# Block 0's attention logits: one product and three split sums instead of eight products, with q, k in strided feature groups

## The chip, the cores and the metric

The kernel runs on one core of a Trainium2 chip. The metric is the device time of one execution in microseconds (us), the median of several runs. Each engine has its own in-order queue: TensorE (PE, with its weight loads PEld), VectorE (DVE), ScalarE (ACT), GpSimd (POOL), and SyncE (SP), which here only issues DMAs.

## The reference, cut to what matters

Two layer types are applied twice each: local attention A, then a gated MLP B (x is 2048 x 1024, 32 heads of 32 features, 8 window positions at a step of 2).

```python
x = x + _A_ref(_layernorm(x), wqkv, wo)
x = x + _B_ref(_layernorm(x), W_gate, W_up, W_down)
...
qkv = (x @ wqkv).reshape(B, S, 3, H, Dh)
idx = pos[:, None] - arange(8) * 2
logits = einsum("bhsd,bhswd->bhsw", q, kg) * scale
o = einsum("bhsw,bhswd->bhsd", softmax(masked logits), vg)
```

A logit is a sum over the 32 features of a head: q of a position times k of the position 0, 2, ... 14 earlier.

## The kernel before, in words

The sequence is cut into four blocks of 512 positions (BLK); a block is four tiles of 128 positions. All order is written by a planner (class Plan, L48). It keeps a plan time for TensorE (`plan.pe`, 0.216 us for each 512-column matmul), puts VectorE's attention chain and its short fixed operations in one order with given durations (`_place_dve`), gives the weight slabs their ring slots (`_place_slabs`), and in the end issues everything sorted by plan time. ACT, POOL and SP have no clock of their own in the plan: their instructions stand in their queues in the order of plan times. Each engine works its queue in order, and an instruction waits for its operands.

**Order on TensorE.** At the start `First` (L278) normalizes block 0 tile by tile while the first slab's matmuls run on finished tiles. Then come the projections of blocks 0 to 3 (`plan_proj`, L354), each six slabs of 512 columns (q, k, v; two halves g), each slab four accumulators j of 128 features x 512 positions, each accumulator 8 matmuls over kc (L364). Between them stands wo of block 0 (`plan_wo`, L633, after block 2), then the MLPs with the other wo's, and layers 2 and 3 in the same way.

**Evictions.** A projection's accumulator is copied to SBUF by ACT (L373) and stored to DRAM in pairs of accumulators (L378, L381, issued from ACT); later the head-major q, k and v are loaded from there by SP (`load`, L492). Block 0's q and k are the exception: `first_logits` (L421) keeps them feature-major in SBUF (`q_fm`, `k_fm`, L433 and L436), so that the logits need no trip to DRAM.

**Block 0's logits before.** For each group c of 128 consecutive features (4 heads), VectorE multiplies q by the eight shifted k (L451: 128 x 4096 bf16). TensorE sums over the features: with a 128 x 32 matrix of ones, cut from `wide` so that group c lands in its 4 head rows, each product takes 8 matmuls (L464), 64 for the eight products, in two lots of 32 (after the first q tile of the second half, and inside block 1's q). They add up in two PSUM banks, which ACT copies out (L473) for the softmax (`soft_a`, `expo`, `soft_b`, L533 to L556).

**Around it.** LayerNorm of block b+1 runs beside the projections of block b (`late_ln`, `plan_ln`, L206): per tile two sums on ACT (L219, L220; S4 to S7 for block 1's tiles and S8 to S11 for block 2's in the text), small operations on VectorE (L226 to L238) and POOL (L233), one normalization on ACT (L244; N4 to N11), and one DMA transpose for two tiles on SP (L250). After the softmax VectorE makes block 0's output in eight groups (L563 to L573), POOL stores each (L574), SP loads it transposed (`load_o`, L582) and TensorE multiplies it by wo (L642).

**Weights.** Layer 0's six slabs stay in SBUF for all four blocks: q's and k's first halves and q's second in `held` (L777, the buffer of the later hT), the rest in the ring of five slots (L190). They are loaded in the order q0 v0 k0 v1 q1 k1, x's tiles between (L785, L771).

Of the kernel before, what the change touches and what calls it, by code (L numbers as in the profile page):

```python
# [14 lines left out]
P = 128  # L15
D = 1024
H = 32
# [13 lines left out]
NG = DH // DG  # L31

# [15 lines left out]
class Plan:  # L48
# [3 lines left out]
    def __init__(self, slots):  # L52
        self.steps = []
        self.pe = 0.0
        self.fixed = []
        self.chain = []
        self.ring = []
        self.slots = slots
        self.n = 0
# [4 lines left out]
    def on_pe(self, n, fn, slabs=()):  # L64
        t = self.pe
        self.at(t, fn)
        self.pe = t + n * MM
        for s in slabs:
            s["last"] = self.pe
        return self.pe  # L70
# [33 lines left out]
    def _place_slabs(self):  # L104
        free = [-10.0] * self.slots
        for s in self.ring:
            free.sort()
            t = max(free.pop(0), s["start"])
            self.at(t + 0.01, s["load"])
            free.append(s["last"])  # L110
# [9 lines left out]
def kernel(  # L120
# [31 lines left out]
    wring = ctx.enter_context(tc.tile_pool(name="wring", bufs=RING))  # L152
# [13 lines left out]
    wide = const.tile([P, 60], BF16, name="wide")  # L166
# [12 lines left out]
    def consts_late():  # L179
        nc.gpsimd.memset(wide[:], 0.0)  # L180
        for hl in range(4):
            nc.gpsimd.memset(wide[32 * hl:32 * hl + 32, 28 + hl:29 + hl], 1.0)
        nc.gpsimd.memset(zpad[:], 0.0)
        for t in (v_d, k_d):
            nc.gpsimd.dma_start(_dram(t[0], 0, [[ROW, P], [P * ROW, KC], [1, HALO]]), zpad[:])
        nc.gpsimd.memset(maskc[:], 0.0)
        for w in range(1, W):
            nc.gpsimd.memset(maskc[:, w, 0:DIL * w], NEG)

    def slab(src_ap, name, start=-10.0):  # L190
        shp = list(src_ap.shape)

        def load():
            t = wring.tile([P, 8, SLAB], BF16, tag="slab", name=name)
            s["t"] = t[:, 0:shp[1], 0:shp[2]]
            nc.sync.dma_start(s["t"], src_ap)

        s = plan.slab(load, start)
        return s
# [154 lines left out]
    def plan_proj(L, b, hooks={}):  # L354
# [3 lines left out]
        def mms(nm, g, j, w, t0=0, t1=TPB, k0=0, k1=KC):  # L358
            def f():
                if t0 == 0 and k0 == 0:  # L360
                    hold[(nm, g, j)] = psum.tile([P, BLK], F32, tag="acc", name=f"acc_{nm}")
                acc = hold[(nm, g, j)]
                for kc in range(k0, k1):
                    nc.tensor.matmul(acc[:, t0 * P:t1 * P], lhsT=w["t"][:, kc, j * P:(j + 1) * P],  # L364
                                     rhs=xnT[(L, b)][:, t0:t1, kc, :], start=(kc == 0), stop=(kc == KC - 1))
            return f
# [20 lines left out]
        tiles = []  # L387
        if L == 0 and b == 0:

            first = First()  # L390
            plan.at(-1.0, first.begin)
            tiles = [("q", 0, j) for j in range(4)]
            for t in range(TPB - 1):
                for h, (nm, g, j) in ((h, x) for h in range(2) for x in tiles):
                    plan.on_pe(1, mms(nm, g, j, w0[(nm, g)], t, t + 1, KC // 2 * h, KC // 2 * (h + 1)), [w0[(nm, g)]])
                    if h == 1 and j == 2:
                        e = plan.on_pe(2, lambda t=t: first.turn(t + 1))
                        plan.at(e, lambda t=t: first.copies(t + 1))
        order = "q0 k0 q1 k1 v0 v1" if "evict" not in hooks else "q0 v0 k0 v1 q1 k1"
        for nm, g in ((o[0], int(o[1])) for o in order.split()):  # L400
            if L == 0:
                w = w0[(nm, g)]
            else:
                col0 = "qkv".index(nm) * D + g * SLAB
                w = slab(wqkv_v[:, :, col0:col0 + SLAB], f"w{nm}_{L}_{b}_{g}")
            for j in range(4):
                if (nm, g, j) in tiles:
                    e = plan.on_pe(2, mms(nm, g, j, w, TPB - 1, TPB), [w])
                else:
                    e = plan.on_pe(8, mms(nm, g, j, w), [w])  # L410
                if "evict" in hooks and nm != "v":
                    hooks["evict"](nm, 4 * g + j, lambda k=(nm, g, j): hold.pop(k), e + T_EV)
                else:
                    plan.at(e + T_EV, evict(nm, g, j))
                if (nm, g, j) in hooks:
                    hooks[(nm, g, j)]()
            ends[nm] = e
        return ends


    def first_logits(st, tm):  # L421
        hold = {}
        Ls = []
# [6 lines left out]
        def evict(nm, c, acc, t):  # L430
            def f():
                if nm == "q":
                    nc.scalar.copy(hold["q"][:, c, :], acc()[:])  # L433
                    return
                kt = hold["k"]
                nc.scalar.copy(kt[:, c, HALO:HALO + BLK], acc()[:])  # L436
                nc.gpsimd.dma_start(_dram(k_d[1], c * P * ROW, [[ROW, P], [1, HALO]]), kt[:, c, BLK:BLK + HALO])
            if nm == "q" and c == 0:
                plan.at(t - 1.0, begin)
            plan.at(t, f)  # L440
            if nm == "k":
                plan.chain.append((lambda: max(t + 0.7, reds.get(c - 4, 0.0) + 0.1), 2.25, mul(c),
                                   (lambda n: tm.__setitem__("logits", n)) if c == KC - 1 else None))

        def mul(c):
            def f():
                if c % 4 < 2:
                    pr = at_pool.tile([P, W, BLK], BF16, tag="pr", name=f"prod_{c}", bufs=2)
                else:
                    pr = tpose.tile([P, W, BLK], BF16, tag="T", name=f"prod_{c}")  # L450
# [5 lines left out]
        def red(c0, n):  # L456
            def f():
                if c0 == 0:
                    Ls.extend(psum.tile([P, 4, P], F32, tag="acc", name=f"L{wh}") for wh in range(2))
                for c in range(c0, c0 + n):  # L460
                    pr = hold.pop(("pr", c))
                    for wh in range(2):
                        for tq in range(TPB):
                            nc.tensor.matmul(Ls[wh][32 * tq:32 * tq + 32, :, :], lhsT=wide[:, 28 - 4 * c:60 - 4 * c],  # L464
                                             rhs=pr[:, 4 * wh:4 * wh + 4, tq * P:(tq + 1) * P],
                                             start=(c == 0), stop=(c == KC - 1),
                                             skip_group_check=True, tile_position=(0, 32 * tq))
            return f

        def out():  # L470
            st["L"] = at_pool.tile([P, W, P], F32, tag="L", name="L_0_0")
            for wh in range(2):
                nc.scalar.copy(st["L"][:, 4 * wh:4 * wh + 4, :], Ls[wh][:])  # L473

        reds = {}

        def step(c0, n):
            def f():
                e = plan.on_pe(1.0 + 2.25 * n, red(c0, n))
                for c in range(c0, c0 + n):  # L480
                    reds[c] = e
                if c0 + n == KC:
                    plan.at(e + T_EV, out)
                    tm["logits_in"] = e + T_EV + 1.5
            return f

        return {"evict": evict, ("q", 1, 0): step(0, 4)}, {("q", 0, 2): step(4, 4)}


    def plan_attn(L, b, ends, st, tm):  # L490
# [106 lines left out]
        def v_ready():  # L597
            t = ends["v"] + 6.0
            if prev:
                t = max(t, prev[-1]["pv"] + 0.5, tm["qk_in"] + 10.0)  # L600
# [17 lines left out]
        def after_pv(t):  # L618
            tm["pv"] = t
            t = max(t + 5.0, st["wo_at"] - 30.0)  # L620
            step = 3.0 if first else PIECE
# [79 lines left out]
    def plan_down(L, b, st, last):  # L701
# [21 lines left out]
        def add(half, t, c0, n):  # L723
            def f():
# [3 lines left out]
                if end:  # L728
                    eng = nc.scalar if t == 1 or (t == TPB - 1 and c0 == SLAB) else nc.sync
                    eng.dma_start(out_dram[r0:r0 + P, c0:c0 + n], xt[:, c0:c0 + n])  # L730
                elif last and half == 1:
                    nc.sync.dma_start(out_dram[r0:r0 + P, :], xt[:])
# [19 lines left out]
    later_hooks = []  # L752

    def proj(L, b):
# [3 lines left out]
        else:  # L758
            hooks = later_hooks.pop() if later_hooks else {}
# [17 lines left out]
    held = hT_pool.tile([P, FC, BLK], BF16, tag="hT", name="wqk_0")  # L777
    for i, (nm, g) in enumerate((("q", 0), ("v", 0), ("k", 0), ("v", 1), ("q", 1), ("k", 1))):
        col0 = "qkv".index(nm) * D + g * SLAB
        if i % 2 == 0:  # L780
            w0[(nm, g)] = {"t": held[:, 4 * i:4 * i + 8, :], "last": 0.0}
            pieces = ((0, KC // 2), (KC // 2, KC)) if i == 0 else ((0, KC),)
            for h, (a, z) in enumerate(pieces):
                plan.at(-7.0 + i + 0.6 * h, lambda w=w0[(nm, g)], a=a, z=z, c=col0:
                        nc.sync.dma_start(w["t"][:, a:z, :], wqkv_v[:, a:z, c:c + SLAB]))  # L785
        else:
            w0[(nm, g)] = slab(wqkv_v[:, :, col0:col0 + SLAB], f"w{nm}_0_{g}", -7.0 + i)
# [7 lines left out]
    for b in range(NB):  # L795
        if b + 1 < NB:
            late_ln(0, b + 1, plan.pe + 9.0, 0.5 if b == 0 else 8.0)
        if b == NB - 1:
            wo(0, 0)
# [56 lines left out]
```

## Time and profile before

| what | us |
|---|---|
| median of 3 runs (1622.80 to 1623.27) | 1623.18 |
| the profiled execution | 1622.84 |
| its span, first to last instruction | 1621.10 |
| TensorE busy in it | 1611.6 |
| reduction of block 0's logits on TensorE, 64 matmuls (chain of waits) | 2 x 1.84 |
| VectorE's eight products, first start to last end | 29.5 to 59.3 |
| ACT busy from 62.70 to 84.85 | 19.67 of 22.15, 33 instructions |
| a group of 32 projection matmuls (chain of waits) | 6.91 |

How to read the profile: the page gives each engine's busy time, the span in 40 slices, and the chain of work that ended last. Groups of instructions are given by line of the kernel, engine, operation and operands (out<-in, partitions x elements). The timeline lists instructions in order of time: start, length, engine, line, operation, and in brackets the idle time before it with what ended it. An instruction's length is not its pitch: matmuls of 379 ns follow each other every 216 ns, and rows of ACT and VectorE can overlap by some 0.1 us.

### The profile page before, as it was taken

What the parts mean: (1) busy time and instruction counts of PE and PEld (TensorE: products, weight loads), DVE (VectorE), ACT (ScalarE), POOL (GpSimd) and SP (SyncE); (2) the same over time, 40 slices, a digit from 0 to 9 for tenths busy, and PEclk for the clock granted to TensorE, in tenths of its full rate; (3) what the DMA queues carried; (4) which work ended last, traced back from release to release, by engine and by line L of the source; (5) the groups of instructions that cost most, each with busy time, mean ns of one, the idle gap of its engine ahead of it and who ended that gap; (6) DMA issues with size and microseconds to landing.
All of it is one profiled execution on the core that took longest, in us unless ns stands there. A gap on an engine that the chain in (4) does not pass through costs nothing.

```text
span 1621.1 us, 19223 instructions
## 1 busy us (share of the span) xinstructions
PE 1611.6 (99%) x7641; PEld 740.6 (46%) x7690; DVE 1014.6 (63%) x1256; ACT 458.1 (28%) x735; POOL 109.3 (7%) x174
## 2 busy tenths in 40 slices
PE   9999999999999999999999999999999999999999
PEld 5444444444444444444444444444444444444444
DVE  4576999989989069960699616986989212211211
ACT  6564421304131241312413251133011311221110
POOL 3221000001001100011000110000000000000000
PEclk9999999999999999999999999999999999999999
DMA  8799798597866988669876699599846655565452
GB/s 240 163 199 192 191 218 210 167 217 193 219 173 211 223 206 208 188 200 234 202 198 196 213 223 226 158 279 240 216 154 194 172 182 162 176 173 165 156 167 67
DMA packets 444203, 314.83 MB, mean 194 GB/s; under 512 B 195504, under 2 KB 438608, under 8 KB 444112
## 3 DMA queue, kind: packets, MB, share of 16 engines
q1 hardware_dynamic: 414944, 281.39, 66.7%
q10 hardware_dynamic: 24368, 23.40, 4.7%
q0 software_dynamic: 4800, 8.80, 1.8%
q8 instruction: 60, 0.98, 0.3%
q14 instruction: 31, 0.25, 0.1%
HBM read 261.77 MB, written 36.05 MB: 184 GB/s over the span
## 4 chain that ended last, share of the span: by engine, by line
PE 99%; DMA 0%; DVE 0%; issue 0%; SPq 0%; POOL 0%; DVEq 0%; POOLq 0%
PE acc_g L672 24%; PE acc_u L672 24%; PE dacc L718 24%; PE acc_v L364 7%; PE acc_k L364 7%; PE acc_wo L642 7%; PE acc_q L364 7%; DMA x<-in_A_x_dram 0%; PE L L464 0%; DVE bst L294 0%; POOL rstd L318 0%; DVE xn_all L323 0%; DVE x L726 0%; SPq L785 0%; DVE xnT L331 0%
## 5 line engine op out<-in xcount | busy, mean ns | idle before, releaser
L672 PE MATMUL acc_u<-xnT,wu 128*128 128x512 bf16 x1792 | 423.3, 379 | 0.0
L672 PE MATMUL acc_g<-xnT,wg 128*128 128x512 bf16 x1792 | 423.3, 379 | 0.0
L718 PE MATMUL dacc<-wd,hT 128*128 128x512 bf16 (+1 forms) x1787 | 386.4, 376 | 1.7
L687 DVE TENSOR_TENSOR hT<-acc_u,r 128x512 bf16<-128x512 f32 x224 | 154.1, 688 | 323.9 <-PE acc_u L672 318.3
L679 ACT ACTIVATE r<-acc_g 128x512 bf16<-128x512 f32 x224 | 133.3, 596 | 711.9 <-PE acc_g L672 700.3
L718 PEld LDWEIGHTS <-hT 128*128 128x128 bf16 x1820 | 178.1, 98 | 209.0
L672 PEld LDWEIGHTS <-wu 128*128 128x128 bf16 x1792 | 175.3, 98 | 211.4
L672 PEld LDWEIGHTS <-wg 128*128 128x128 bf16 x1792 | 175.3, 98 | 211.5
L512 DVE TENSOR_TENSOR pr<-qhm,khm 128x4096 bf16<-128x4096 bf16 x56 | 127.9, 2284 | 30.7 <-DMA khm<-k_d 30.6
L563 DVE TENSOR_TENSOR pvt<-a,vhm 128x4096 bf16<-128x4096 bf16 x64 | 146.2, 2285 | 0.2
L522 DVE TENSOR_TENSOR l<-l,pr 128x1024 f32<-128x1024 f32 x112 | 136.8, 1221 | 2.2
L726 DVE TENSOR_TENSOR x<-dacc,x 128x512 bf16<-128x512 f32 (+1 forms) x65 | 43.2, 681 | 126.1 <-PE dacc L718 125.9
L364 PE MATMUL acc_v<-xnT,wv 128*128 128x512 bf16 x512 | 112.0, 379 | 0.0
L642 PE MATMUL acc_wo<-wo,oT 128*128 128x512 bf16 x496 | 111.0, 379 | 0.8
L364 PE MATMUL acc_k<-xnT,wk 128*128 128x512 bf16 x384 | 84.8, 379 | 0.0
L219 ACT ACTIVATE xn_all<-x 128x1024 bf16<-128x1024 bf16 x60 | 63.3, 1055 | 73.8 <-DVE x L649 71.0
L571 DVE TENSOR_TENSOR pvt<-pvt 128x2048 bf16<-128x2048 bf16 x64 | 78.1, 1221 | 1.3
L373 ACT CAST stage_q<-acc_q 128x512 bf16<-128x512 f32 x56 | 32.0, 582 | 162.1 <-PE acc_q L364 153.3
L642 PEld LDWEIGHTS <-oT 128*128 128x128 bf16 x512 | 50.1, 98 | 60.4
L364 PEld LDWEIGHTS <-wv 128*128 128x128 bf16 x512 | 50.1, 98 | 60.2
L244 ACT ACTIVATE xn_all<-x,nb,rstd 128x1024 bf16<-128x1024 bf16 x60 | 71.9, 1233 | 14.2 <-DVE nb L238 11.2
L574 POOL DMA_DIRECT2D o_d<-ohm x64 | 35.2, 550 | 599.7 <-DVE ohm L573 581.7
(76 smaller groups left out, 883.1 us busy)
## 6 DMA issues: line engine op xcount, KB each, us to landing
wg<-in_B_W_gate_dram SPq DMA_DIRECT2D x56, 1024.0 KB, 7.2
wu<-in_B_W_up_dram SPq DMA_DIRECT2D x56, 1024.0 KB, 5.4
wd<-in_B_W_down_dram SPq DMA_DIRECT2D x48, 1024.0 KB, 6.4
wo<-in_A_wo_dram SPq DMA_DIRECT2D x16, 1024.0 KB, 6.9
wv<-in_A_wqkv_dram SPq DMA_DIRECT2D x10, 1024.0 KB, 5.7
wk<-in_A_wqkv_dram SPq DMA_DIRECT2D x9, 1024.0 KB, 5.0
vhm<-v_d SPq DMA_DIRECT2D x32, 284.0 KB, 7.0
v_d<-stage_v ACTq DMA_DIRECT2D x32, 256.0 KB, 6.8
```

What stands on the lines that cost most here:

```text
L219: nc.scalar.activation(junk, xt[:], ACT.Identity, accum_out=st[:, 0, t % 2:t % 2 + 1])
L244: nc.scalar.activation(hold["xn"][:, t, :], x_tiles[b * TPB + t][:], ACT.Identity, scale=rstd[:, i:i + 1], bias=nb[:, i:i + 1])
L364: nc.tensor.matmul(acc[:, t0 * P:t1 * P], lhsT=w["t"][:, kc, j * P:(j + 1) * P], rhs=xnT[(L, b)][:, t0:t1, kc, :], start=(kc == 0), stop=( ...
L512: nc.vector.tensor_tensor(pr[:], st["q"][:], _ap(st["k"], HALO - DIL * w, [[HALO + P, DH], [1, P]]), op=ALU.mult)
L522: nc.vector.tensor_tensor(l[:], pr[:, 0:8] if i == 0 else l[:], pr[:, 8 * i + 8:8 * i + 16], op=ALU.add)
L563: nc.vector.tensor_tensor(tt[:], a_bc, v_sh, op=ALU.mult)
L571: nc.vector.tensor_tensor(tt[:, 0:4], tt[:, 0:4], tt[:, 4:8], op=ALU.add)
L642: nc.tensor.matmul(acc[:], lhsT=st["oT"][:, c, t, :], rhs=ws[half]["t"][:, c, :], start=(c == 0), stop=(c == KC - 1))
L672: nc.tensor.matmul(acc[:], lhsT=w["t"][:, kc, (j % 4) * P:(j % 4 + 1) * P], rhs=xnT[(L, b)][:, :, kc, :], start=(kc == 0), stop=(kc == KC ...
L679: nc.scalar.activation(r[:], hold.pop(("g", j))[:], ACT.Relu)
L687: nc.vector.tensor_tensor(st["hT"][:, j, :], hold.pop(("u", j))[:], hold.pop(("r", j))[:], op=ALU.mult)
L718: nc.tensor.matmul(accs[(t, c0)][:], lhsT=st["hT"][:, j, t * P:(t + 1) * P], rhs=w["t"][:, jl, c0 - half * SLAB:c0 - half * SLAB + n], sta ...
```

## The change: what it does

1. In block 0, group c of q and k now holds every eighth feature: c, c+8, c+16, ... (the weights are read by TensorE with a step of eight columns). Partition p of every group then belongs to head p // 4, so products of different groups may be added partition by partition.
2. VectorE adds the products of groups 0 to 6 in f32 (two halves of 128 x 2048, `lacc`), and splits the sum into three bf16 terms: ACT copies it to bf16 (term_0), VectorE subtracts, ACT copies the rest (term_1), VectorE subtracts again (term_2). TensorE sums the last product (group 7) and the three terms with one 128 x 32 matrix: 32 matmuls in one lot, placed after the second v tile of block 1. The terms take the buffers of the products, of k_fm and of q_fm.
3. Block 0's order is v's first half, then q and k group by group, then v's second half; `First` works with v's slab. q and k are loaded whole (two halves of 1 MB, rows of 2 KB) ahead of block 1's x tiles. The ring is one tile with numbered slots; k takes two of them, reserved until its last use.
4. wo of block 0 stands inside block 3's projections, six accumulators later. Its inputs are loaded 1.2 plan us apart instead of 3.0, and block 1's v loads follow them.
5. In the last layer each half row of the output is stored when it is done, in all blocks.

```diff
-    wring = ctx.enter_context(tc.tile_pool(name="wring", bufs=RING))
+    wring = ctx.enter_context(tc.tile_pool(name="wring", bufs=1))
...
-    wide = const.tile([P, 60], BF16, name="wide")
+    wide = const.tile([P, H], BF16, name="wide")
+    ring = wring.tile([P, 8 * RING, SLAB], BF16, name="ring")
...
+                    if L == 0 and b == 0 and nm != "v":
+                        lhsT = _ap(w["t"], kc * D + 4 * g + j, [[D // P, P]])
...
+            steps = [("v", 0, j) for j in range(4)] + [("q", 0, 0), ("q", 0, 1), ("k", 0, 0), ("k", 0, 1)]
+            steps += [(nm, c // 4, c % 4) for c in range(2, KC) for nm in "qk"] + [("v", 1, j) for j in range(4)]
...
             if nm == "k":
-                plan.chain.append((lambda: max(t + 0.7, reds.get(c - 4, 0.0) + 0.1), 2.25, mul(c),
-                                   (lambda n: tm.__setitem__("logits", n)) if c == KC - 1 else None))
+                plan.chain.append((lambda: t + 0.7, 2.3, mul(c), None))
+                for h in range(2 if 0 < c < KC - 1 else 0):
+                    plan.chain.append((lambda: 0.0, 2.3, add(c, h), split(0, h) if c == KC - 2 else None))
+                if c == KC - 1:
+                    for n in range(2):
+                        for h in range(2):
+                            plan.chain.append((lambda n=n, h=h: tm[("split", n, h)], 2.3, rest(n, h),
+                                               split(1, h) if n == 0 else (lambda now: tm.__setitem__("logits", now))))
...
+                nc.vector.tensor_tensor(acc[:], hold[("pr", 0)][:, ws] if c == 1 else acc[:], hold[("pr", c)][:, ws], op=ALU.add)
...
+                nc.scalar.copy(terms[n][:, 4 * h:4 * h + 4], hold[("acc", h)][:])
+
+            def after(now):
+                t = max(now + 0.2, tm.get(("split", n, 0), 0.0))
+                plan.at(t, f)
+                tm[("split", n, h)] = t + 2.4
...
+                nc.vector.tensor_tensor(acc[:] if n == 0 else terms[2][:, 4 * h:4 * h + 4], acc[:],
+                                        terms[n][:, 4 * h:4 * h + 4], op=ALU.subtract)
...
+            for n, term in enumerate([hold[("pr", KC - 1)]] + terms):
+                for wh in range(2):
+                    for tq in range(TPB):
+                        nc.tensor.matmul(Ls[wh][32 * tq:32 * tq + 32, :, :], lhsT=wide[:],
+                                         rhs=term[:, 4 * wh:4 * wh + 4, tq * P:(tq + 1) * P],
...
-        return {"evict": evict, ("q", 1, 0): step(0, 4)}, {("q", 0, 2): step(4, 4)}
+        return {"evict": evict}, {("v", 0, 1): step}
...
-            step = 3.0 if first else PIECE
+            step = 1.2 if first else PIECE
...
-                if end:
-                    eng = nc.scalar if t == 1 or (t == TPB - 1 and c0 == SLAB) else nc.sync
+                if last:
+                    eng = nc.scalar if end and (t == 1 or (t == TPB - 1 and c0 == SLAB)) else nc.sync
                     eng.dma_start(out_dram[r0:r0 + P, c0:c0 + n], xt[:, c0:c0 + n])
-                elif last and half == 1:
-                    nc.sync.dma_start(out_dram[r0:r0 + P, :], xt[:])
...
+    wo_hook = {("k", 0, 1): lambda: wo(0, 0)}
...
+    for nm, at in (("q", -6.0), ("k", -5.5)):
...
+            plan.at(at, lambda w=full, c=col0, a=KC // 2 * g, z=KC // 2 * (g + 1):
+                    nc.sync.dma_start(w[:, a:z, :], wqkv_v[:, a:z, c:c + D]))
```

## The prediction, made before the change was run

> **What bounds the kernel now.** I read the page first: the engine shares, the 40 slices, the chain that ended last.
>
> ```profile
> PE 1611.6 (99%) x7641; PEld 740.6 (46%) x7690; DVE 1014.6 (63%) x1256; ACT 458.1 (28%) x735; POOL 109.3 (7%) x174
> ...
> PEclk9999999999999999999999999999999999999999
> ...
> PE 99%; DMA 0%; DVE 0%; issue 0%; SPq 0%; POOL 0%; DVEq 0%; POOLq 0%
> ```
>
> TensorE is the path from end to end. Of 1621.1 us it lacks 9.5, nearly all in the first 16 us. So a gain must come out of TensorE's own instructions, and any wait put in front of them is paid in full. ACT's 28% is a mean; the stage decides.
>
> Next the timeline of 0 to 70 us, for the instructions that the change takes out:
>
> ```profile
> 40.79 1.91 PE L464 MATMUL L<-prod,wide 128*32 128x512 bf16 x32
> ...
> 50.36 8.90 DVE L451 TENSOR_TENSOR prod<-q_fm,k_fm 128x4096 bf16<-128x4096 bf16 x4 [10.43 <-ACT k_fm L436]
> ...
> 60.00 1.91 PE L464 MATMUL L<-prod,wide 128*32 128x512 bf16 x32
> ```
>
> Two lots of 32 reduction matmuls; the chain of waits charges 1.84 us each. Then ACT alone, 62 to 85 us (block 1's projections; it normalizes block 2 there):
>
> ```profile
> 66.51 1.06 ACT L219 ACTIVATE xn_all<-x 128x1024 bf16<-128x1024 bf16 x1
> 67.47 0.19 ACT L219 ACTIVATION_READ_ACCUMULATOR xn_all<-x 128x1 f32 x1
> 67.70 1.06 ACT L220 ACTIVATE xn_all<-x 128x1024 bf16<-128x1024 bf16 x1
> 68.66 0.19 ACT L220 ACTIVATION_READ_ACCUMULATOR xn_all<-x 128x1 f32 x1
> 68.75 1.04 ACT L545 ACTIVATE L<-L 128x1024 f32<-128x1024 f32 x1
> 69.70 0.56 ACT L373 CAST stage_k<-acc_k 128x512 bf16<-128x512 f32 x1
> 70.29 0.37 ACTq L381 DMA_DIRECT2D k_d<-stage_k  x1
> 70.70 0.58 ACT L373 CAST stage_k<-acc_k 128x512 bf16<-128x512 f32 x1 [0.44 <-PE acc_k L364]
> 71.18 1.06 ACT L219 ACTIVATE xn_all<-x 128x1024 bf16<-128x1024 bf16 x1
> ```
>
> The reader is to see one row ending where the next begins: from 62.70 to 84.85 us ACT is full, though its share of the kernel is 28%. Last, the groups by form, for prices:
>
> ```profile
> L522 DVE TENSOR_TENSOR l<-l,pr 128x1024 f32<-128x1024 f32 x112 | 136.8, 1221 | 2.2
> ...
> L364 PEld LDWEIGHTS <-wqk 128*128 128x128 bf16 x480 | 41.8, 98 | 44.1 <-issue 1.9 <-DMA wqk<-in_A_wqkv_dram 0.9
> ...
> L473 ACT COPY L<-L 128x512 f32<-128x512 f32 x2 | 1.1, 588 | 1.1 <-PE L L464 1.1
> ```
>
> **The change, part by part.** Removed: 64 reduction matmuls become 32 (one product, three terms). TensorE gains 1.84 us. That is all there is to gain.
>
> VectorE: 8 products stay (2.2 us pitch in the row at 50.36). Added are 12 adds and 4 subtractions of 128x2048 in f32. f32 rows cost 691 ns at 512 and 1226 at 1024 (softmax rows), so 535 per 512 more: 2.29 at 2048. 16 of them make 37 us, hidden only while TensorE doesn't ask.
>
> ACT: four copies of 128x2048 f32 to bf16. From 588 at 512 and 1040 at 1024 (the exp row) 2048 gives 1.95; back to back a row starts 0.09 before the last ends, so a pitch of 1.86.
>
> Where they land. In plan time block 0 ends at 42.77; real time is 10.2 later (the first four tiles end at 8.21 in the plan, at 18.41 in the chain of waits). Block 1's q and k take 16 tiles of 1.727 us (6.91 a group) from 53.0, then two v tiles, so TensorE reaches the reduction at 84.0 and without a wait ends it at 85.9. By the plan's own times (VectorE's chain worked through with its 2.3s and the LayerNorm's small operations) the four copies stand at 57.8, 60.8, 66.3 and 68.8; block 2's LayerNorm sums S8 to S11 at 52.1 to 60.2, its norms N8 to N11 at 62.8 to 67.7. So all eight LayerNorm steps stand ahead of the last copy in ACT's queue, and the plan books no time on ACT. S8 stands behind the eviction of block 1's fifth tile, which TensorE ends at 61.7: ACT can't start earlier.
>
> ACT from there, with pitches of the rows above: S8 starts 62.2. A sum pair takes 2.24 (66.51 to 68.75), a norm 1.14, an eviction 0.48, one with its DMA issue 1.0 (69.70 to 70.70). S8 to S10 with three evictions (two with an issue): 6.72+2.48, to 71.4. VectorE's sixth add should be done at about 71 (second product at 31.5, then 6.75 us a group and three sets of small operations), so the first copy runs at once, to 73.3. Eviction, S11, eviction with issue: 77.0. Second copy 78.9. Two evictions, N8, N9, one eviction: 83.1. Third copy 85.0. N10, eviction with issue, N11: 88.3. Fourth copy 90.2. VectorE's last subtraction: 92.5. TensorE's last four matmuls: 92.8.
>
> A second way to the same figure: before, ACT went from S8's start to N11's end in 22.15 us with ten evictions and the exp. Less exp (0.95) and one eviction (0.5), plus four copies (7.5): 28.2 after 62.2, so 90.4.
>
> The **wait** is thus 92.8 - 85.9 = 6.9 us. Behind the waiting matmuls stand six v tiles of block 1; nothing else can fill TensorE, which works in order. The cover of ACT's copies is gone in just this stage. Bounds for the copy: four 512 casts at their pitch of 0.48 (1.92) or the bare f32 slope (0.88 x 2 = 1.76); over four copies that is 0.5 us. If x rows land late (next paragraph) VectorE's start moves the whole by up to 2.
>
> Loads at the start: ahead of the last half of k lie 5 MB, as before ahead of v's second slab, now 6 MB in all. The DMA view moves 336 to 367 GB/s from 5 to 20 us. Six MB end near 20.5, land some 1.3 later, and TensorE needs that half at 22.7: nothing, at worst 1 us. Rows of 2 KB instead of 1 KB can only help (no row shows the weights so). The four x tiles of block 1 now come behind k and land at 21 to 27 instead of 17 to 19. ACT's first sums wait, but ACT is idle from 38 to 62 for 64% of the time, which takes that up.
>
> v first: the same 1 MB in the same two halves stands ahead; nothing. wo six tiles later: o's last product in the before-trace ends 50.9 us after its softmax starts, 2.8 of them a wait for ACT that falls away. Softmax at 94.1 gives 142; the o write lands in 5.1 (median), the o load in 3.9: 151. wo starts at 148.3+6.9 = 155. Nothing; cover 4 us. SP's q loads wait for the reduction (term_2 lies in their buffer), with one transpose of block 2 queued behind them; released at 92.8 it lands near 98, needed at 103. Attention of block 1 started at 136.3 before and was held by k loads; now at 142, against a path 5 us later: nothing. Half stores: twelve more SP issues, off the path. `wide` by affine_select: 0.3 us on an idle POOL.
>
> Weights of q and k read with a step of eight elements: 128 loads. The nearest row is 98 ns for the same 128 columns, under a matmul pitch of 216; I take 0. At the start 28 load-matmul pairs of 128 columns ran in 1.83 us, so a packed load needs at most 65 ns; it must grow over threefold to be seen. At eightfold (each element by itself) it costs 128 x (523 - 216) = 39 us.
>
> Sum: -1.84 + 6.9 = +5.1. The profiled execution took 1622.84 (span 1621.10 and 1.74 around): 1627.9. The median stands 0.34 higher: **1628.2**.
>
> **Rivals.**
> *The copies come in time* (14%): the reduction finds its terms ready; 1623.18 - 1.84 = 1621.3. For it speaks that the plan has the last term at 73.5 and the reduction at 73.9. Against it: ACT would need to be 6.9 us quicker in a stretch that the trace shows full.
> *The clock falls in the wait* (20%): TensorE would stand idle from 85.2 to 90.2. The trace shows TensorE cold only at its start: 42 warm-up matmuls at 96 ns each, later 128-column pairs at 65. Were that repaid once, it costs 42 x 31 ns = 1.3 us, or half of those 4.04 us, 2: 1629.5 to 1630.2. The Trainium skill (TensorE: Matmul & The Clock Gate, Part 1) says that one idle window of about 3.4 us halves the clock. By that rule an idle of 5 us hits about every second run; no run here shows it yet, so I give it the smaller chance.
> *The strided weights are slow* (3%): decided from 216 ns a load; up to 1661. The Trainium skill (SBUF — State Buffer, Door 1) speaks of 16-byte lines and a penalty for each access that enters a new line, which is this step exactly. The Trainium skill also says (TensorE: Matmul & The Clock Gate, Weight-path perf modes) that fast weight load allows column steps up to 1,024 elements. No run here shows either.
> *Late k, late x or a late o adds 1 to 4 us* (4%): up to 1632.
> Slower by at most 0.2% through a shorter wait (6%): 1623.5 to 1626.4.
> The forecast keeps 53%, 1626.4 to 1629.5.
>
> **Numbers.** Range: from 1623 to 1632, which leaves out the first rival and the strided weights (17%) and a little at the top. 0.2% is 3.2 us, about what a measurement of this kernel can tell from no change. Slower by more: forecast, clock, strided, late, 80%. Within: the first rival but for 2%, and the shorter wait, 18%. Faster by more: those 2%, since 1.84 is all there is.
>
> **What would show it.** In the after-trace: TensorE waiting near 85 to 92 us for ACT's copy and VectorE's last subtraction; ACT without idle from 62 to 92, the fourth copy behind N11; reduction rows of 1.84 us in all; weight loads of q and k at 98 ns; matmuls behind the wait at 216 ns pitch (if 430, the clock fell). I am wrong if ACT takes the copies ahead of the LayerNorm, or if a copy costs well under 1.7 us.

## The result and the profile after

The changed kernel takes **1630.76 us** (median of 6 runs, 1629.93 to 1634.18), the kernel before 1622.99 (6 runs, 1622.57 to 1623.27): a ratio of 1.0051, 95% interval 1.0038 to 1.0064. Its profiled execution took 1630.63 us with a span of 1628.8, 7.7 more than the span of before.

First the page: engine shares, granted clock by slice, and the chain that ended last.

```profile
PE 1615.7 (99%) x7658; PEld 746.9 (46%) x7658; DVE 1051.0 (65%) x1272; ACT 466.6 (29%) x739; POOL 114.8 (7%) x172
...
PEclk9999999999999999999999999999999999999999
...
PE 94%; DVE 2%; DMA 1%; ACT 1%; issue 1%; SPq 0%; POOL 0%; ACTq 0%; DVEq 0%
```

TensorE's share is as before, but it is busy 4.1 us longer though it has 32 reduction matmuls fewer (some 2.5 us of this is no work: before's page has 49 matmul records fewer than weight loads, 7641 to 7690, and its trace shows gaps where they are missing), and only 94% of the chain is TensorE's: the way back from the end now leaves it for DVE, ACT and DMA. The clock row shows nothing wrong, and it misleads: a slice is 40.7 us long, so half speed over 7 us still leaves a 9. Next TensorE's waits (us in total, times, the longest):

```profile
PE L L512 <- ACT term L490: 4.9, 2, 4.7
...
PE L L512 <- DVE term L503: 1.3, 1, 1.3
PE acc_q L375 <- DMA xnT<-xn_all: 1.2, 1, 1.2
```

L512 is the reduction, L490 ScalarE's copies to bf16, L503 VectorE's subtractions: they hold TensorE for 6.2 us. The third row is a wait of block 3's first projection for its transposed input. All three are new. The timeline of TensorE around the reduction and at block 3's start:

```profile
83.64 0.61 PE L512 MATMUL L<-prod,wide 128*32 128x512 bf16 x8
84.08 0.60 PE L512 MATMUL L<-term,wide 128*32 128x512 bf16 x8
84.95 0.40 PE L512 MATMUL L<-term,wide 128*32 128x512 bf16 x4 [0.26 <-ACT term L490]
90.03 1.04 PE L512 MATMUL L<-term,wide 128*32 128x512 bf16 x8 [4.68 <-ACT term L490]
92.36 0.62 PE L512 MATMUL L<-term,wide 128*32 128x512 bf16 x4 [1.28 <-DVE term L503]
92.92 5.07 PE L375 MATMUL acc_v<-xnT,wqv 128*128 128x512 bf16 x16
97.82 7.07 PE L375 MATMUL acc_v<-xnT,ring 128*128 128x512 bf16 x32
104.73 7.07 PE L375 MATMUL acc_q<-xnT,wqv 128*128 128x512 bf16 x32
...
147.51 7.07 PE L375 MATMUL acc_q<-xnT,wqv 128*128 128x512 bf16 x32 [1.18 <-DMA xnT<-xn_all]
```

TensorE is at the reduction at 83.64 and leaves it at 92.98. Behind the waits eight reduction matmuls take 1.04 us where eight took 0.61, and 16 projection matmuls 5.07. The stretches of TensorE (busy time, count, granted clock, DMA share, GB/s) say why:

```profile
84.00:88.00 4.00, 1.09 (x20) 1.00 0.81 176
88.00:92.00 4.00, 1.04 (x8) 0.63 0.09 25
92.00:96.00 4.00, 3.64 (x12) 0.52 0.59 171
96.00:100.00 4.00, 4.00 (x21) 1.00 0.97 180
```

The granted clock fell to one half in the wait and came back by 96. Read in steps of 0.1 us it stood at 0.50 from 89.05 to 95.9, for 6.8 us.

ScalarE in that stretch (the rows that begin block 2's LayerNorm, the four copies, and the last norm):

```profile
61.78 1.06 ACT L225 ACTIVATE xn_all<-x 128x1024 bf16<-128x1024 bf16 x1
...
71.42 1.90 ACT L490 CAST term<-lacc 128x2048 bf16<-128x2048 f32 x1 [0.33 <-DVE lacc L481]
...
76.95 1.90 ACT L490 CAST term<-lacc 128x2048 bf16<-128x2048 f32 x1 [0.44 <-ACT stage_q L384]
...
83.00 1.90 ACT L490 CAST term<-lacc 128x2048 bf16<-128x2048 f32 x1
...
86.96 1.24 ACT L250 ACTIVATE xn_all<-x,nb,rstd 128x1024 bf16<-128x1024 bf16 x1 [0.45 <-ACT stage_k L384]
88.10 1.88 ACT L490 CAST term<-lacc 128x2048 bf16<-128x2048 f32 x1
```

The four copies, 7.6 us of work, are spread from 71.42 to 89.98, because ScalarE takes its queue in order and the sums, norms and evictions stand between them. VectorE meanwhile waits for the copies:

```profile
84.93 2.29 DVE L503 TENSOR_TENSOR term<-lacc,term 128x2048 bf16<-128x2048 f32 x1 [1.52 <-ACT term L490]
90.02 2.29 DVE L503 TENSOR_TENSOR term<-lacc,term 128x2048 bf16<-128x2048 f32 x1 [2.79 <-ACT term L490]
```

Last the weight loads of block 0's q and k, by form, with the step of eight columns (busy us, mean ns, idle):

```profile
L375 PEld LDWEIGHTS <-ring 128*128 128x128 bf16 x68 | 9.6, 141 | 5.1
L375 PEld LDWEIGHTS <-wqv 128*128 128x128 bf16 x64 | 9.1, 143 | 4.5
```

**The balance.** Block 2's first matmul stood at 98.11 before and stands at 104.73: 6.6 later. The 48 matmuls between reduction and block 2 (92.98 to 104.89, the end of the pipeline counted) took 11.91 us; at 216 ns they take 10.37. So 1.5 of the 6.6 are the clock behind the reduction, and 5.1 the longer reduction (with its own matmuls at half clock) less the saved matmuls and a start that was 0.3 earlier. With 1.2 for block 3's wait this makes 7.8; the spans differ by 7.7.

### The profile page after: what moved, and what is told of

It reads as the page before. It is cut to its first block, busy times and chain, and to the rows that moved or that the text cites. A ratio compares the mean times of both kernels' runs of the same rounds, so it can differ in the third digit from the quotient of the medians.

```text
span 1628.8 us, 19258 instructions
## 1 busy us (share of the span) xinstructions
PE 1615.7 (99%) x7658; PEld 746.9 (46%) x7658; DVE 1051.0 (65%) x1272; ACT 466.6 (29%) x739; POOL 114.8 (7%) x172
## 4 chain that ended last, share of the span: by engine, by line
PE 94%; DVE 2%; DMA 1%; ACT 1%; issue 1%; SPq 0%; POOL 0%; ACTq 0%; DVEq 0%
PE acc_u L711 24%; PE acc_g L711 24%; PE dacc L757 24%; PE acc_wo L681 7%; PE acc_v L375 5%; PE acc_q L375 5%; PE acc_k L375 5%; DVE lacc L481 1%; DMA x<-in_A_x_dram 1%; DVE prod L471 1%; DMA xnT<-xn_all 0%; SPq L825 0%; POOL rstd L239 0%; ACT xn_all L225 0%; ACT term L490 0%
## 5 line engine op out<-in xcount | busy, mean ns | idle before, releaser
L711 PEld LDWEIGHTS <-ring 128*128 128x128 bf16 x3584 | 350.7, 98 | 422.9
L711 PE MATMUL acc_g<-xnT,ring 128*128 128x512 bf16 x1792 | 423.3, 379 | 0.0
L711 PE MATMUL acc_u<-xnT,ring 128*128 128x512 bf16 x1792 | 423.3, 379 | 0.0
L757 PE MATMUL dacc<-ring,hT 128*128 128x512 bf16 (+1 forms) x1820 | 388.1, 376 | 0.0
L375 PEld LDWEIGHTS <-ring 128*128 128x128 bf16 x1152 | 115.6, 100 | 133.0
L375 PE MATMUL acc_k<-xnT,ring 128*128 128x512 bf16 x512 | 114.1, 379 | 0.0
L681 PE MATMUL acc_wo<-ring,oT 128*128 128x512 bf16 x512 | 111.8, 379 | 0.0
L375 PE MATMUL acc_v<-xnT,ring 128*128 128x512 bf16 x384 | 84.2, 379 | 0.0
L239 POOL TENSOR_TENSOR rstd<-vpe,neg_half 128x2 f32<-128x2 f32 x30 | 37.0, 1235 | 552.9 <-DVE vpe L237 400.8
```

Of the source, the lines that this page charges most:

```text
L375: nc.tensor.matmul(acc[:, t0 * P:t1 * P], lhsT=lhsT, rhs=xnT[(L, b)][:, t0:t1, kc, :], start=(kc == 0), stop=(kc == KC - 1))
L681: nc.tensor.matmul(acc[:], lhsT=st["oT"][:, c, t, :], rhs=ws[half]["t"][:, c, :], start=(c == 0), stop=(c == KC - 1))
L711: nc.tensor.matmul(acc[:], lhsT=w["t"][:, kc, (j % 4) * P:(j % 4 + 1) * P], rhs=xnT[(L, b)][:, :, kc, :], start=(kc == 0), stop=(kc == KC ...
L757: nc.tensor.matmul(accs[(t, c0)][:], lhsT=st["hT"][:, j, t * P:(t + 1) * P], rhs=w["t"][:, jl, c0 - half * SLAB:c0 - half * SLAB + n], sta ...
```

## The experiments

The theory: ScalarE's queue order in the stretch 62 to 90 us sets the end of the reduction, the clock falls in the wait, and block 3's wait is a third item. Rivals: VectorE's f32 adds set the end; the strided weight loads cost time; a later place of the reduction would be enough. All edits are to the changed kernel unless another is named. A single execution differs from its kernel's median by up to some us, so single ones are read for their traces.

**e3: fewer adds on VectorE.**

```diff
+                if c >= 3:
+                    return
```

> VectorE leaves out the adds of groups 3 to 6 (8 adds of 2.25 us, so the sum lacks four of the eight products); the plan keeps their times, so every queue keeps its order. Rival V (VectorE's adds are the bound): the last term comes up to 18 us earlier, the wait at the reduction is gone, 1622 to 1624. Theory A (ScalarE's queue is the bound): the first copy can start at most 0.3 us earlier, since ScalarE reaches it at 71.1 anyway; the wait stays at 5.5 to 6.2 us and the time at 1630 to 1631.

Measured: 1630.46 us (1630.08 to 1631.05), ratio 1.0046 (1.0031 to 1.0061); waits 4.7 for ScalarE and 1.3 for VectorE, as in the changed kernel. Eight adds of 2.29 us taken away change nothing: with ScalarE's queue as it is, VectorE's sum isn't the bound, and that rival falls.

**e2 and e8: LayerNorm of block 2 earlier**, so that its steps come ahead of ScalarE's copies (two norms still stand between the first copy and the second). One kernel, run twice.

```diff
-            late_ln(0, b + 1, plan.pe + 9.0, 0.5 if b == 0 else 8.0)
+            late_ln(0, b + 1, plan.pe + (2.0 if b == 1 else 9.0), 0.5 if b == 0 else 8.0)
```

> Block 2's LayerNorm is planned 7 us earlier (plan time of block 1's start plus 2 instead of plus 9); nothing else is changed. Theory A (the term copies stand behind block 2's eight LayerNorm steps in ScalarE's queue): the sums then run from about 55 us, beside evictions, and all eight steps are over before the first copy can start at 71; VectorE's own chain sets the end, the last subtraction ends at 86 to 88 instead of 92.3, TensorE's wait at the reduction falls from 6.2 to 1 to 2.5 us, the clock does not fall, and the time is 1624 to 1626. Rival V (VectorE's adds are what comes late, ScalarE only follows): the wait stays above 5 us, and the time at 1629 to 1631.

Measured: 1630.78 us (1626.30 to 1633.28), ratio 1.0053 (1.0036 to 1.007). The profiled execution is the lowest of the four, and its timeline has the wait cut to 3.4 us:

```profile
85.00 0.82 PE L512 MATMUL L<-term,wide 128*32 128x512 bf16 x12
87.54 0.61 PE L512 MATMUL L<-term,wide 128*32 128x512 bf16 x8 [1.72 <-ACT term L490]
89.87 0.40 PE L512 MATMUL L<-term,wide 128*32 128x512 bf16 x4 [1.71 <-DVE term L503]
```

The order on ScalarE does move the wait, though less than expected. The last matmuls start at 89.87 instead of 92.36, so the last term is there 2.5 us earlier. TensorE also reached the reduction 0.9 later (84.56), after 1.3 us of waiting for a weight load at the start of this execution, which shortens its wait without a gain. The next bound stands right behind: VectorE's sum ends at 73.6, the first copy starts at 73.8, and copies and subtractions follow each other from there. So block 2's steps in ScalarE's queue hold the last term back by 2.5 us, not by the whole wait. And the median didn't follow: why?

> The kernel of the early LayerNorm once more, for a second profiled execution: its first was 1626.3 while three others took 1630.2 to 1633.3 with a mean clock of 0.998. If the spread comes from the two waits that are left (3.4 us at the reduction in two pieces, 1.1 at block 3), a slower execution shows one of them past 3 us in one piece, and the clock below 1 behind it.

Measured, one execution: 1630.24 us. Its timeline and its stretches:

```profile
85.06 0.40 PE L512 MATMUL L<-term,wide 128*32 128x512 bf16 x4 [0.33 <-ACT term L490]
87.88 0.61 PE L512 MATMUL L<-term,wide 128*32 128x512 bf16 x8 [2.42 <-ACT term L490]
90.20 0.62 PE L512 MATMUL L<-term,wide 128*32 128x512 bf16 x4 [1.71 <-DVE term L503]
90.76 6.35 PE L375 MATMUL acc_v<-xnT,wqv 128*128 128x512 bf16 x16
```

```profile
88.00:92.00 4.00, 2.29 (x15) 0.68 0.39 131
92.00:96.00 4.00, 4.00 (x11) 0.50 0.89 198
96.00:100.00 4.00, 4.00 (x20) 0.96 0.58 203
```

Here TensorE came in time, waited 4.5 us in all, and 2.42 and 1.71 us of idle with matmuls between them were enough for half the clock: 16 matmuls in 6.35 us, 3.63 at full clock (e2). In e2's profiled execution 1.72 and 1.71 were not, and it was 3.9 us shorter, 2.7 of them in these 16 matmuls. Of e2's four executions the lowest has a mean clock of 1.000, the other three (1630.18 to 1633.28) have 0.998. So in most executions the clock still falls behind the shorter wait and takes its gain back; what else moved those three isn't seen, as they have no trace.

**e9: the changed kernel once more.**

> The changed kernel once more. Theory A: the wait at the reduction is 6.2 us again within 0.5, the clock falls behind it again, and what varies between executions (1629.9 to 1634.2) is the wait for block 3's transposes, 0.8 to 4 us.

Measured: 1630.10 us, waits 4.7, 1.3 and 1.0. The picture repeats.

**e5: the wait filled with work.** 21 matmuls without use, into a spare accumulator, ahead of the wait for term_1's second half.

```diff
+                    if (n, wh) == (2, 1):
+                        scratch = psum.tile([P, BLK], F32, tag="acc", name="fill")
+                        for i in range(21):
+                            nc.tensor.matmul(scratch[:], lhsT=ident[:], rhs=terms[0][:, 0:4, 0:P], start=True, stop=True)
```

> 21 matmuls of 128x512 that nobody reads fill TensorE's queue between the first and the second half of the second term, 4.5 us in the wait. If the idle wait is what lowers the clock: the granted clock stays at 1.00, the 16 v matmuls behind the reduction take 3.6 us instead of 5.07 and the reduction's end comes up to 0.5 us earlier; 1628.5 to 1629.5. If the clock falls for another reason: the same 1630.8 as the changed kernel, with the clock at 0.5 from 92 to 96 us. If the fillers themselves delay the reduction: more than 1631.

Measured: 1630.19 us (1628.69 to 1632.37), ratio 1.0046 (1.0031 to 1.0061). The profiled execution, 1628.69:

```profile
85.43 4.71 PE L514 MATMUL fill<-term,ident 128*128 128x512 bf16 x21
90.19 0.61 PE L516 MATMUL L<-term,wide 128*32 128x512 bf16 x8
92.51 0.40 PE L516 MATMUL L<-term,wide 128*32 128x512 bf16 x4 [1.71 <-DVE term L503]
92.84 3.63 PE L375 MATMUL acc_v<-xnT,wqv 128*128 128x512 bf16 x16
```

The reduction ends when it did (92.9), so the fill takes nothing away from the wait; but the 16 matmuls behind it take 3.63 us, not 5.07. This prices the clock's fall by itself, in one trace against another: about 1.5 us. The medians (1630.19 and 1630.76) lie too close in their spreads to show it, and 1630.19 is above the time that was expected. Two of the four executions have a mean clock of 0.999, the other two 1.000.

**e4: only the reduction (and wo) later.**

```diff
-        return {"evict": evict}, {("v", 0, 1): step}
+        return {"evict": evict}, {("v", 1, 3): step}
...
-            step = 1.2 if first else PIECE
+            step = 1.2 if L == 0 and b <= 1 else PIECE
...
-    wo_hook = {("k", 0, 1): lambda: wo(0, 0)}
+    wo_hook = {("k", 1, 1): lambda: wo(0, 0)}
```

> The reduction stands after block 1's last v tile, 6 tiles (10.4 us) later; so that its inputs can be there, wo of block 0 stands 8 tiles later, and block 1's o loads 1.2 plan us apart. Theory A: the last term comes at 92 to 93 us as before, the reduction stands at 94, so its wait is gone and the granted clock stays at 1.00; that gives back 6.2 us of waiting and about 2 of slow clock. The wait for block 3's transposes then grows, since TensorE gets there 8.9 us earlier: by 2 us if the transposes follow TensorE's pace, by up to 9 if they do not. Together 1624 to 1630. Rival: what is late follows TensorE (evictions that the copies stand behind), so the wait moves along with the reduction and stays at 5 us or more, with the clock falling again: 1630 or more.

Measured: 1639.13 us (1638.36 to 1646.05), ratio 1.0109 (1.0088 to 1.013): a miss, and the dearest kernel of all. The wait at the reduction is gone, and two others took its place:

```profile
PE acc_q L375 <- DMA xnT<-xn_all: 9.2, 2, 7.6
PE acc_g L711 <- DMA xnT<-xn_all: 4.0, 1, 4.0
```

The issues on SP, in order, show the first:

```profile
96.35 0.54 SPq L537 DMA_DIRECT2D qhm<-q_d  x1
97.00 3.86 SPq L256 DMA_TRANSPOSE xnT<-xn_all  x1
```

SP's first q load goes into the buffer of term_2, so it waits until the reduction has read that term (96.3), and block 2's second transpose stands behind it in SP's queue. The norms that it needs were done by 88.3. TensorE needs that transpose at 96.3 and gets it at 103.9. The clock didn't stay at 1.00 either: it stood at 0.50 for 10.2 us from within this wait on and for 3.4 at the end of the one of 4.0. The reduction can't be moved back freely: a load that has nothing to do with block 2 hands its wait on.

**e7: block 3's x and LayerNorm earlier.**

```diff
-            plan.at(-4.5 if b == 1 else 41.5 * (b - 1) + 1.0 * (t % TPB), load_x(t))
+            plan.at((0.0, -4.5, 41.5, 64.0)[b] + (b > 1) * 1.0 * (t % TPB), load_x(t))
...
-            late_ln(0, b + 1, plan.pe + 9.0, 0.5 if b == 0 else 8.0)
+            late_ln(0, b + 1, plan.pe + (9.0, 9.0, -6.0)[b], (0.5, 8.0, 0.5)[b])
```

> The changed kernel, but block 3's x tiles are loaded earlier and its LayerNorm and transposes are planned 15 and 7.5 us earlier. Theory A's second term (wo's later place lets TensorE reach block 3 before its transposes): the wait of 1.2 us at block 3 goes, the one at the reduction stays at 6 us or grows by a us (a LayerNorm step of block 3 may stand ahead of the logits' copy): 1629 to 1630.5, and executions closer together than 1629.9 to 1634.2. If the wait at block 3 has nothing to do with that order it stays, 1630.8.

Measured: 1629.19 us (1629.02 to 1630.26), ratio 1.004 (1.0026 to 1.0054). Block 3's wait is gone and those at the reduction are unchanged, so that item is one by itself, worth 1.2 us in the trace and 1.6 between the medians (0.9 against e9's one execution on the same chip).

**e6: all together.** Block 2's and block 3's x tiles and LayerNorm early, wo's weights later, the reduction three v tiles later, wo two tiles later.

```diff
-        return {"evict": evict}, {("v", 0, 1): step}
+        return {"evict": evict}, {("v", 1, 0): step}
...
-        ws = [slab(wo_v[:, :, h * SLAB:(h + 1) * SLAB], f"wo_{L}_{b}_{h}", 30.0) for h in range(2)]
+        ws = [slab(wo_v[:, :, h * SLAB:(h + 1) * SLAB], f"wo_{L}_{b}_{h}", 50.0) for h in range(2)]
...
-    wo_hook = {("k", 0, 1): lambda: wo(0, 0)}
+    wo_hook = {("k", 0, 3): lambda: wo(0, 0)}
...
-            plan.at(-4.5 if b == 1 else 41.5 * (b - 1) + 1.0 * (t % TPB), load_x(t))
+            plan.at((0.0, -4.5, 36.0, 64.0)[b] + (b > 1) * 1.0 * (t % TPB), load_x(t))
...
-            late_ln(0, b + 1, plan.pe + 9.0, 0.5 if b == 0 else 8.0)
+            late_ln(0, b + 1, plan.pe + (9.0, 0.5, -6.0)[b], (0.5, 2.0, 0.5)[b])
```

> Everything that theory A names as late is moved: block 2's LayerNorm starts with block 1 (plan +0.5), its x tiles are loaded 5 plan us earlier and wo's weights 20 later; block 3's x and LayerNorm come earlier too, with its transposes ahead of most of block 1's k loads; the reduction stands three v tiles later (after the first of v's second half), wo of block 0 two tiles later. Theory A: the first copy starts at 71 or before, the last term is done at 86 to 88, the reduction stands at 88.8, no wait there, none for block 3's transposes, clock 1.00; what is left is the saved 1.84 us and a start 0.3 earlier: 1620.9 to 1622, against 1622.96 before. Rival V (VectorE is the bound, whatever the order): a wait of 3 us or more stays at the reduction, 1624 or more. If the waits for transposes come from the DMA queue itself and not from the order in it, the time stays loose, 1623 to 1630.

Measured: 1621.81 us (10 runs, nine of them 1621.03 to 1622.24, one 1624.80), before 1623.13, ratio 0.9994 (0.9985 to 1.0003). The profiled execution is the one of 1624.80; in it the reduction runs without a wait. The last subtraction ends at 89.6 instead of 92.3, so the early LayerNorm gives 2.7 us, and the later place of the reduction (89.34 instead of 83.64) covers the rest. One new wait is left:

```profile
153.86 15.67 PE L681 MATMUL acc_wo<-ring,oT 128*128 128x512 bf16 x64 [2.07 <-DMA oT<-o_d]
```

```profile
150.00:154.00 4.00, 1.93 (x10) 1.00 0.84 209
154.00:158.00 4.00, 4.00 (x12) 0.57 1.26 241
```

A wait of 2.07 us again took the clock with it: 64 matmuls in 15.67 us, 13.98 in the changed kernel.

**e10: wo two tiles later still**, on top of e6, to take that wait away.

```diff
-    wo_hook = {("k", 0, 3): lambda: wo(0, 0)}
+    wo_hook = {("q", 1, 1): lambda: wo(0, 0)}
```

> The kernel with everything early, and wo of block 0 two tiles (3.45 us) later still, after the second q tile of block 3's second half. Its one wait in the profiled execution was 2.1 us for block 0's o loads at wo (and a slow clock behind it). If that was the last wait: none is left behind the start, all executions lie together, and the time is the kernel before less 1.84 us and up to 0.3 at the start: 1620.8 to 1621.5 against 1623.1, faster by 0.08 to 0.14%. If the next consumer (block 0's LayerNorm and transposes ahead of the MLP) becomes late by it: a wait at the first gate tile near 195 us, 1622 to 1625.

Measured: 1630.31 us (1627.83 to 1630.83), ratio 1.0039 (1.0025 to 1.0053): a miss. wo no longer waits, but the MLP behind it does:

```profile
PE acc_g L711 <- DMA xnT<-xn_all: 7.4, 1, 7.4
```

```profile
184.43 1.17 SPq L202 DMA_DIRECT2D ring<-in_B_W_gate_dram  x1
185.72 0.57 SPq L202 DMA_DIRECT2D ring<-in_B_W_up_dram  x1
187.17 8.94 SPq L256 DMA_TRANSPOSE xnT<-xn_all  x1
```

wo makes block 0's new x, which is normalized and transposed for the MLP. With wo two tiles later, the second transpose is issued behind two slabs of 1 MB and lands 13.4 us after its issue (187.17 to 200.6). In e6 both transposes were issued from 178.29 on, the second at 182.1, ahead of the slabs, and landed after 5.2 and 8.5. That the slabs make the landing longer is argued from this order; no run moves the slabs alone.

**e11: the weights of q and k without the step**, on top of e10.

```diff
-                        lhsT = _ap(w["t"], kc * D + 4 * g + j, [[D // P, P]])
+                        lhsT = _ap(w["t"], kc * D + (4 * g + j) * P, [[1, P]])
```

> The same kernel, but block 0's q and k read their weights packed (128 neighbouring columns) instead of every eighth; the sums over features then mix heads, so the output is not the reference's. The strided loads of the changed kernel took 141 ns instead of 98 and stood under matmuls of 216 ns pitch. Theory: hidden, so no difference, within 0.3 us of the kernel it is compared with, and loads of 98 ns in 18 to 45 us. Rival (the stride costs time on the path): 128 loads of 43 ns, up to 5.5 us faster than its twin.

Measured: 1629.44 us (1628.69 to 1630.69) against e10's 1630.31 on the same chip; the spreads overlap, the medians lie 0.9 apart where 0.3 was expected, and the wait for the transpose is 8.2 here instead of 7.4. So the times can't settle it; the traces can. The loads themselves:

```profile
L375 PEld LDWEIGHTS <-ring 128*128 128x128 bf16 x67 | 6.6, 98 | 7.9
L375 PEld LDWEIGHTS <-wqv 128*128 128x128 bf16 x64 | 6.2, 98 | 7.3
```

98 ns instead of 138 to 144: the step costs some 43 ns a load. They lie under the pitch of 216: in the changed kernel's trace block 0's tiles with strided weights start every 1.73 us (24.84, 26.57, 28.30, ...), and four of block 1's tiles with packed weights take 6.91, which is 1.73 each.

**e12: block 3's LayerNorm 2 us later than in e6**, so that a pair of sums comes behind ScalarE's copy of the logits.

```diff
-            late_ln(0, b + 1, plan.pe + (9.0, 0.5, -6.0)[b], (0.5, 2.0, 0.5)[b])
+            late_ln(0, b + 1, plan.pe + (9.0, 0.5, -4.0)[b], (0.5, 2.0, 0.5)[b])
```

> The kernel of e6_all_early with one number changed: block 3's layer norms planned 2 us later (offset -4 instead of -6), so that a pair of ScalarE sums that ran at 94.7-96.8, ahead of the copy of the logits at 96.9, comes behind it. Theory: the 2.07 us wait of the out projection at 153.86 is the only wait left behind the start in e6_all_early's profiled execution, and it comes from block 0's attention chain, which the sums held up by 2 x 1.06 + 2 x 0.19 = 2.5 us, and with it o's stores and loads. Without it no wait is left, the granted clock is 1.00 through 150 to 160 and the time is 1620.8 to 1621.6 with no execution near 1624.8; against before's 1623.1 that is a ratio of 0.9985 to 0.999. Rival: o's loads are late for a reason that lies in the DMA queue and not in ScalarE; then the wait of about 2 us at wo stays, the median is again about 1621.8 and single executions reach 1624 to 1625.

Measured: **1621.03 us** (11 runs, 1620.48 to 1622.82), before 1622.86 (15 runs, 1622.45 to 1623.20), ratio 0.9991 (0.9982 to 1.0). All of TensorE's waits in its profile:

```profile
PE warm L295 <- POOL neg_half L182: 1.4, 1, 1.4
PE acc_v L375 <- ACT xnT L337: 0.5, 2, 0.2
PE acc_v L375 <- DVE xnT L337: 0.3, 1, 0.3
```

The copy of the logits moved from 96.90 to 93.43 (2.2 us of it the two sums, 1.2 an eviction ahead of it that waited less), wo starts at 151.24 without a wait, and nothing is left behind the start. That the sums alone made e6's wait isn't shown: nine of e6's ten runs lie as low as these, and this profile is of the lowest of the eleven. From the first full tile to the first tile of the MLP TensorE takes 174.62 us here (18.06 to 192.68), before 176.56 (18.25 to 194.81): 1.94 less, which is what the 32 matmuls saved (1.84) within 0.1. The medians lie 1.83 apart; the interval reaches 1.0, and ten of the eleven runs lie below every run of before.

## Why the prediction was right, and where its parts were off

*What bounds the kernel.* Right that TensorE is the path, but the 9.5 us that it lacks are not "nearly all in the first 16 us": 3.5 are there, 3.4 behind 1600 us, nearly all after its last matmul, and 2.5 are gaps of missing records.

*The saving, 1.84.* Right: with every wait gone (e12) it is what is left, 1.94 in the trace.

*The wait at the reduction, 6.9.* Right in mechanism and size. ScalarE's chain was worked out from 62.2 to 90.2 and ran from 61.78 to 89.98, each of the four copies within 0.2 us of its place; that it began 0.4 early was made up by 0.33 of waiting for VectorE's sixth add, which ended at 71.4 (about 71 foretold). The last subtraction ended at 92.31 (92.5 foretold) and the reduction at 92.98 (92.8); at full clock its last four matmuls, 0.40 instead of 0.62, would have ended at 92.76. TensorE stood idle for 6.2 us; in the prediction's terms (the end less the end without a wait) the wait was 7.4, since TensorE came at 83.64 and not at 84.0, and some of its reduction ran at half clock. That the sum still came out is the earlier start making up for this. e3 shows that VectorE's adds don't set the end, e2, e8 and e6 that ScalarE's order does, but for 2.5 to 2.7 us only. With most of block 2's steps out of the way TensorE still waits 4.5 us (e8): VectorE's sum is there at 73.6 (e2), and the copies, block 1's evictions between them and the subtractions follow each other on two engines. The prediction laid the whole wait to ScalarE's queue and didn't look how close behind it the next bound stands.

*The clock in the wait.* Held for a rival at 20%, at 1.3 to 2 us. It came true in addition to the forecast: 1.5 us. That this lies in the priced range is partly luck: the price was taken from the warm-up matmuls at 96 ns, and the granted clock is 1.00 in their stretch (1.4 to 5.5 us), so no row shows them at half clock. 1627.9 + 1.5 + 1.2 (block 3's wait, next) gives 1630.6 for the profiled execution, which took 1630.63; the agreement to a tenth is partly luck, by the two errors just named. The Trainium skill (TensorE: Matmul & The Clock Gate, Part 1) has one idle window of about 3.4 us halve the clock; the idle of 4.68 us here agrees, with 0.52 behind it. But the clock also fell behind 2.07 us (e6) and behind 2.42 and 1.71 (e8), so that 3.4 isn't a wait that is safe. The step that failed was the chance: "an idle of 5 us hits about every second run" was too low. All six executions of the changed kernel, e9's one and all nine of e3 and e7, which have the same wait, show a mean clock of 0.997 or 0.998; before shows 1.000.

*wo six tiles later: "Nothing; cover 4 us".* This step failed. o's loads were in time as worked out (issued 149.30, wo at 157.87 without a wait), but the step looked only at wo's own input. With wo gone from its old place TensorE comes to block 3 at 146.3 instead of 153.5, and block 3's transposes, issued from 136.95 on (137.93 before, so no later), landed at 147.5: 1.2 us of wait (e7 takes it away). What a moved step uncovers has to be counted as well as what it needs.

*The start, nothing to 1 us.* Right: the first full tile stands at 17.93 instead of 18.25, 0.3 earlier. That is chance: in the other traces of this start it stands at 17.8 to 18.9, with 0 to 1.3 us of waiting for the first weights. From 10 to 20 us the loads, now with rows of 2 KB, moved 397 to 403 GB/s, before 358 to 367, and k's last half landed at 21.2 (21.8 by the prediction's sum). Block 1's x tiles and ScalarE's first sums cost nothing.

*Strided weight loads, 0.* Right in its cost, wrong in "at 98 ns": 141 to 143, under the 216 that was named as the bound. The Trainium skill (SBUF — State Buffer, Door 1) speaks of a penalty for each new 16-byte line; a step of 16 bytes costs 43 ns here for 128 columns, and no time.

*Prices.* Copies 1.90 (1.95 foretold), the next row 1.80 behind their start (1.86), adds and subtractions 2.29 (2.29).

*Left open.* Why the clock fell in e8 (2.42 and 1.71 us idle) and not in e2 (1.72 and 1.71): no run separates the length of the waits from their place. The traces give a hint that it is the place as well. Read in steps of 0.1 us, every stretch at 0.50 that began in or behind such a wait is a whole multiple of 3.41 us long: 3.41 in e6, 6.83 in the changed kernel, e7, e8, e9, e10 and e11, 10.24 in e3, 10.24 and 3.41 in e4. In e4 the two falls lie 109.2 us apart, 32 times 3.41. So the clock seems to be set at ticks 3.41 us apart, by how much TensorE stood idle since the last one: 2.07 of 3.41 us before the fall in e6, 2.8 in e8. Whether a wait of 2 us is caught would then hang on where a tick falls in it; this wasn't tested.

## What to carry to other kernels

When work is moved from a full engine to "idle" ones, write out the in-order queue of the receiving engine in that stretch, with what stands between the new steps: a share of 28% over the kernel says nothing about it. For each step that moves, ask three things: what it waits for, what now comes earlier because it is gone, and what is queued behind it on the DMA queues. A wait of 2 us or more on TensorE can cost nearly as much again in clock (e6: 2.07 and 1.7), so a wait is better taken away wholly than shortened.

## What the runs showed of the hardware

- In and behind waits of 2.07 to 8.2 us the granted clock stood at 0.50 for 3.4, 6.8 or 10.2 us and then at 1.00 again; the row of matmuls behind waits of 2.07 to 4.69 us took 1.2 to 2.7 us longer. Behind 1.71 us (e5), or 1.72 and 1.71 (e2), it stayed at 1.00.
- A weight load of 128 columns with a step of eight bf16 elements takes 141 to 143 ns, packed 98.
- A DMA transpose issued behind two loads of 1 MB landed after 13.4 us (e10), ahead of them after 5.2 and 8.5 (e6).
- A DMA that waited for its buffer held what stood behind it in SP's queue: a transpose whose input was ready by 88.3 was issued at 97.0, and TensorE waited 7.6 us for it (e4).
